# A recurrent-memory attention block with a SwiGLU gate, forward and backward: the phases around its two loops rebuilt

## The chip, the cores and the metric

The kernel runs on one core of a Trainium2 chip. The metric is device time in microseconds (us) from the first to the last instruction of one execution. A profile of an execution lists, for each engine, when it worked and what it waited for. The engines are TensorE (PE: matmuls; its weight loads are listed as PEld), VectorE (DVE), ScalarE (ACT), GpSimd (POOL) and SyncE (SP, which here only starts transfers). SBUF is the core's working memory with 128 partitions, PSUM the small memory into which PE writes, DRAM the large one outside. A DMA is a transfer between them; ACT, SP and POOL start the DMAs in this kernel.

## The reference

The reference computes an output and then, by automatic differentiation, the gradients of nine inputs, which are outputs too. The forward part, cut to what matters:

```python
xn = layernorm(x)                                   # x: 2048 tokens x 640
# A: 64 segments of 32 tokens, one after the other, 8 memory rows carried on
for s in range(64):
    h = concat([mem, xn[32*s:32*s+32]])             # 40 rows x 640
    q, k, v = h @ Wq, h @ Wk, h @ Wv                # 32 heads of 128: 4096 columns each
    p = softmax(mask(q @ k.T * scale))
    o = (p @ v) @ Wo                                # 40 x 640
    mem = o[:8]
    outs.append(o[8:])
s = concat(outs)
# B: SwiGLU, F = 1728
z = (silu(xn @ w1) * (xn @ w3)) @ w2
g = silu(z)
out = x + s * g
```

All inputs and outputs are bf16. The outputs are `out` and the gradients of x, mem0, Wq, Wk, Wv, Wo, w1, w3 and w2 for a given `grad_out` (G).

## The kernel before

The program is a row of phases, each with its own SBUF and PSUM pools. `k.dma` starts a DMA on SP and ACT in turn; `k.copy(..., eng='v' or 's')` copies on DVE or ACT. A pool's `bufs` is how many buffers a tile name rotates through.

```python
phase1_ln(k)          # LayerNorm; stores xn as rows (XN) and transposed (XNT)
phase2_Bfwd(k)        # SwiGLU forward; stores gate, up, h, z, g, G*g (GS), its transpose (GST)
phase3_Afwd(k)        # projections of the first tokens, then the forward loop over 64 segments
phase3b_out(k, out_0) # O projection of all tokens, out, and G*s (GG)
phase4_Abwd(k, out_2) # GO projection of the last tokens, a prologue, the backward loop over 64 segments
phase6_Awgrads(k, out_3, out_4, out_5, out_6)  # gradients of Wq, Wk, Wv, Wo; gradient of xn from attention
phase5_Bbwd_ln(k, out_1, out_7, out_8, out_9)  # SwiGLU backward, LayerNorm backward, gradients of w1, w3, w2
```

Phase 2, per chunk of 128 columns of F and 512 tokens:

```python
nc.scalar.activation(sig, pg, Sigmoid)          # pg, pu: PSUM, fp32
nc.vector.tensor_copy(gt, pg)
nc.scalar.copy(ut, pu)
nc.vector.tensor_tensor(sl, gt, sig, mult)
nc.vector.tensor_tensor(hBT[:, fc, :], sl, ut, mult)
k.dma(k.GATET[...], gt);  k.dma(k.UPT[...], ut)
# ... (z, g and the rows of h for each 128 tokens)
emit_wT_B(k, w1s, w3s, w2s, ps1, "pht")         # transposes of w1, w3, w2 through one PSUM buffer
```

Phase 3 begins by loading its four weights, projects 672 tokens, then loops; at the end of each segment the new memory, transposed, is stored element by element:

```python
for (W, src) in ((Wv, k.A_Wv), (Wk_, k.A_Wk), (Wq, k.A_Wq)):
    k.dma(W[:], src...)                          # 5.2 MB each
k.dma(Wo[:], k.A_Wo...)
for xt in range(6):                              # 112 tokens each
    for W in (Wv, Wk, Wq): ...                   # 8 banks of 512 columns, 5 matmuls each
# ... forward loop, at the end of segment t:
nc.gpsimd.dma_start(k.MTD[:, :, (t + 1) * 8:(t + 2) * 8], nxt[:, :, 0:8])
```

The O projection works tile by tile of 96 tokens, tokens as the stationary operand; the backward phase then loads its transposed weights and starts:

```python
for h in range(H):                               # 32 heads
    matmul(pa, oT[:, h, :], Wo[:, h, 0:512]);  matmul(pb, oT[:, h, :], Wo[:, h, 512:640])
# ... phase 4
k.dma(WoT[:], k.WOT...)                          # then WvT, WkT, WqT: 5.2 MB each
```

Phase 6, for 8 groups of 4 heads and 22 tiles of up to 120 rows (24 memory rows and 96 tokens):

```python
mem_rows(k, [(k.MTD, k.MR), (k.GMT, k.GMR)])     # memory rows turned back by PE
for qd in range(8):
    for tl in range(22):
        # loads of dS, P and the rows of k, q, g
        # transposes of dS (t6); three row gradients r6p -> gr (ACT, DVE, ACT)
        # their transposes t6g -> gT (ACT, DVE, ACT), then the gradient of xn:
        for i in range(3):
            for j in range(4):
                matmul(g5, gT[:, i, j, :], W[:, j, 0:512]);  matmul(g1, gT[:, i, j, :], W[:, j, 512:640])
        # acc[tile] += g5, g1 (DVE)
    for i in range(3):                           # gradients of Wv, Wk, Wq: 5 banks, 22 x 5 matmuls
        # ... always the same five PSUM banks
# then gWo: gow = rows(GMR, GS) in 44 loads; per group one load of orr; 704 pairs of matmuls
```

Phase 5:

```python
for ps_i in range(npass):                        # w2 gradients: 5 passes over all tokens
    for tt in range(16):
        k.dma(hb[...], k.HB[tt*128:(tt+1)*128])  # the rows of h loaded again in each pass
        # up to 6 matmuls
for fc in range(14):
    for blk in range(4):                         # 512 tokens
        # 5 matmuls -> pghb; loads of gate and up; 2 ACT and 7 DVE operations
        k.dma(GUPT[...], gupT);  k.dma(GGATET[...], ggT)
for tt in range(16):                             # loads of GGATET, GUPT; 56 pairs of matmuls; LayerNorm backward
    ...
for srcT in (GGATET, GUPT):                      # w1, w3 gradients: loaded again, transposed by PE, then matmuls
    ...
```

Of the kernel before, what the change touches and what calls it, by code (L numbers as in the profile page):

```python
# [40 lines left out]
class K:  # L41
# [110 lines left out]
    def setup_dram(self):  # L152
# [8 lines left out]
        self.GATET = mk("GATET", (self.FC * P, S))  # L161
        self.UPT = mk("UPT", (self.FC * P, S))
        self.HB = mk("HB", (S, self.FC * P))
        self.ZB = mk("ZB", (S, D))
# [3 lines left out]
        self.GG = mk("GG", (S, D))  # L168
        self.GXA = mk("GXA", (S, D))
# [20 lines left out]
        self.MTD = mk("MTD", (P, self.DC, T * 8))  # L190
        self.GMT = mk("GMT", (P, self.DC, T * 8))
        self.MR = mk("MR", (T * 8, D))
        self.GMR = mk("GMR", (T * 8, D))
# [25 lines left out]
    def tok_src(self, x0, nx, w, c0, c1):  # L219
# [4 lines left out]
        while a < nx:  # L224
            t, r = divmod(x0 + a - self.NB0, 24)
            if r == 0 and nx - a >= 48 and c1 - c0 <= 1024:
                nt = (nx - a) // 24
                out.append((a, a + 24 * nt, self.step_src(w, t, t + nt, 8, 32, c0, c1)))
                a += 24 * nt
            else:  # L230
                m = min(24 - r, nx - a)
                out.append((a, a + m, self.step_src(w, t, t + 1, 8 + r, 8 + r + m, c0, c1)))
                a += m
        return out
# [119 lines left out]

def fold_turn(k, bank, fs):
# [10 lines left out]
def phase3_Afwd(k):  # L366
    nc, tc = k.nc, k.tc
    D, DC, S, H, HD, T = k.D, k.DC, k.S, k.H, k.HD, k.T
    with tc.tile_pool(name="aw", bufs=1) as wp:
        Wv = wp.tile([P, DC, HD], BF16, name="Wv")  # L370
        Wk_ = wp.tile([P, DC, HD], BF16, name="Wk")
        Wq = wp.tile([P, DC, HD], BF16, name="Wq")
        Wo = wp.tile([P, H, D], BF16, name="Wo")
        for (W, src) in ((Wv, k.A_Wv), (Wk_, k.A_Wk), (Wq, k.A_Wq)):
            k.dma(W[:], src.rearrange("(dc p) h e -> p dc (h e)", p=P))
        k.dma(Wo[:], k.A_Wo.rearrange("h e d -> e h d"))


        units = wT_A_units(k, Wq, Wk_, Wv, Wo)
        with tc.tile_pool(name="b0", bufs=2) as io, tc.tile_pool(name="b0s", bufs=3) as stp, \  # L380
                tc.tile_pool(name="b0p", bufs=4, space=bass.MemoryType.PSUM) as ps, \
                tc.tile_pool(name="b0q", bufs=2, space=bass.MemoryType.PSUM) as ps2:
            ui = 0
            for xt in range(6):
                x0 = 112 * xt
                xs = io.tile([P, DC, 112], BF16, name="b0x", tag="b0x")
                nc.sync.dma_start(xs[:], k.XNT[:, x0:x0 + 112].rearrange("(dc p) t -> p dc t", p=P))
                for wi, (W, dst) in enumerate(((Wv, k.QVX[:, 1]), (Wk_, k.KX[:, :]), (Wq, k.QVX[:, 0]))):
                    for cg in range(4):
                        st = stp.tile([112, 1024], BF16, name="b0st", tag="b0st")  # L390
                        for b in range(2):
                            c0 = cg * 1024 + b * 512
                            pb = ps.tile([112, 512], F32, name="b0pb", tag="b0pb")
                            for dc in range(DC):
                                nc.tensor.matmul(pb[:], xs[:, dc, :], W[:, dc, c0:c0 + 512],
                                                 start=(dc == 0), stop=(dc == DC - 1))
                            k.copy(st[:, b * 512:(b + 1) * 512], pb[:], eng='vs'[b])
                        nc.sync.dma_start(dst[x0:x0 + 112, cg * 1024:(cg + 1) * 1024], st[:])
                        nu = ((xt * 12 + 4 * wi + cg + 1) * len(units)) // 72
                        while ui < nu:  # L400
                            units[ui](ps2, "wTps", stp)
                            ui += 1

        with tc.tile_pool(name="ast", bufs=1) as st, tc.tile_pool(name="achain", bufs=1) as ch, \
                tc.tile_pool(name="afill", bufs=1) as fl, \
                tc.tile_pool(name="aps", bufs=1, space=bass.MemoryType.PSUM) as ps, \
                tc.tile_pool(name="apm", bufs=1, space=bass.MemoryType.PSUM) as psm:
            kTs = [st.tile([P, H, 120], BF16, name=f"kT{i}") for i in range(2)]
            vt = st.tile([40, HD], BF16, name="vt")
            hxs = [st.tile([P, DC, 32], BF16, name=f"hx{i}") for i in range(2)]  # L410
            qTs = [st.tile([P, 4, P], BF16, name=f"xqT{i}") for i in range(2)]
            xPs = [st.tile([120, 4, P], BF16, name=f"xP{i}") for i in range(3)]
            PTs = [st.tile([120, 4, P], BF16, name=f"xPT{i}") for i in range(2)]
            for tt in kTs + hxs + qTs + xPs + PTs:
                nc.gpsimd.memset(tt[:], 0.0)
            bA, bB, bC = [psm.tile([P, 512], F32, name=f"bank{i}") for i in range(3)]
            pm = bA
            with nc.allow_non_contiguous_dma(reason="tiny mem0 transpose load"):
                for dc in range(DC):
                    nc.sync.dma_start(hxs[0][:, dc, 0:8], k.mem0[:, dc * P:(dc + 1) * P].rearrange("m p -> p m"))  # L420
                nc.sync.dma_start(k.MTD[:, :, 0:8], hxs[0][:, :, 0:8])
            rides = {}
            WARM = dict(G2=2, G3=1, G4=2, G5=2)

            def ride_ld(t):
                x0 = k.NB0 + 24 * t
                b, sub = t // 4, t % 4
                if sub == 0 and x0 < S:
                    w = min(96, S - x0)
                    rt = ch.tile([P, DC, 96], BF16, name="ride", tag="ride")  # L430
                    nc.sync.dma_start(rt[:, :, 0:w], k.XNT[:, x0:x0 + w].rearrange("(dc p) s -> p dc s", p=P))
                    rides[b] = (rt, w)

            def ride(t):
                x0 = k.NB0 + 24 * t
                if x0 >= S:
                    return
                b, sub = t // 4, t % 4
                rt, w = rides[b]
                r0 = 24 * sub  # L440
                r1 = min(r0 + 24, w)
                nc.gpsimd.tensor_copy(hxs[t % 2][:, :, 8:8 + r1 - r0], rt[:, :, r0:r1])

            def chain(t, gap):
                tl, s = t // 3, t % 3
                hx = hxs[t % 2]
                kT = kTs[tl % 2]

                def half(W, b, sg, eng):
                    bank = (bA, bB)[b]  # L450
                    packed_half(k, bank, hx, W, b)
                    k.copy(sg[:, b * 512:(b + 1) * 512], bank[:], eng=eng)
# [311 lines left out]
def phase4_Abwd(k, out2):  # L764
# [3 lines left out]
    with tc.tile_pool(name="gw", bufs=1) as wp:  # L768
# [27 lines left out]
        with tc.tile_pool(name="gst", bufs=1) as st, tc.tile_pool(name="gchain", bufs=1) as ch, \  # L796
# [25 lines left out]
            def ride_ld(t):  # L822
                if t < 8:
                    return
# [860 lines left out]
```

## Time and profile before

| what | value |
|---|---|
| time, median of 3 | 6446.4 us (6438.1 to 6450.8) |
| span of the profiled execution | 6484.5 us |
| granted PE clock, mean | 0.911 |
| forward loop with its tail | 614 to 1994 us |
| backward loop | 2436 to 3768 us |

The other phases, from the first and last start of their lines: LayerNorm 0 to 66, phase 2 from 66 to 281, weight transposes to 346, first projections 375 to 589, O projection 1994 to 2224, GO projection to 2327, prologue to 2436, phase 6 from 3848 to 5512, gWo 5546 to 5746, w2 gradients to 5999, SwiGLU backward to 6149, LayerNorm backward to 6287, w1 and w3 gradients to the end.

How to read the views. In a table of stretches, a row is a stretch of time with the busy time of each engine in it. In a list of waits, a row is "who waited <- for whom: us in total, times, longest". In a list of groups, a row is the source line, engine, operation, output<-input, shape and count, then "busy us, mean ns of one", then the idle time just before and what ended it. An engine's idle time costs something only where that engine sets the end of its stage. "L90" and "L92" are the two copy helpers, whatever phase they serve.

### The profile page before, as it was taken

The numbers are of one execution on the slowest core, as the hardware profiler recorded it, in microseconds if no ns is written. First come the engines' busy times: TensorE is split into PE (matmuls) and PEld (weight loads), VectorE is DVE, ScalarE is ACT, GpSimd is POOL, SyncE is SP. The second block draws the span as 40 slices with busy tenths as digits, with TensorE's granted clock in tenths as the row PEclk, the third lists the DMA queues.
The fourth block names the chain that finished last, engine by engine and source line by source line (L and its number), as shares of the span: only waits on it lengthen the run. The fifth ranks groups of instructions, "written<-read, shape, count | busy, mean of one in ns | idle before, by whom it ended". The sixth has DMA issues, their size and how long they took to land. (4 is left out here: it accounts for less than half of the span.)

```text
span 6484.5 us, 167849 instructions
## 1 busy us (share of the span) xinstructions
PE 5360.5 (83%) x68068; PEld 3158.2 (49%) x68620; DVE 2423.8 (37%) x7541; ACT 1896.1 (29%) x5180; POOL 990.0 (15%) x1507
## 2 busy tenths in 40 slices
PE   6868999999978748888889849889998999765698
PEld 3445555555545425555556525555555554432244
DVE  5423555555542124444444412322223222020852
ACT  3323455554542122322233212322223222010301
POOL 0000344343341012332333200000000000000000
PEclk9879999999988968998899969999999999875899
DMA  6474454444455555665566552332233222665673
GB/s 190 155 254 152 122 138 137 133 133 129 132 160 134 175 151 149 170 162 155 160 171 179 143 92 75 98 79 75 77 85 89 76 80 67 147 173 171 199 170 92
DMA packets 1053670, 880.57 MB, mean 136 GB/s; under 512 B 528584, under 2 KB 944168, under 8 KB 1046944
## 3 DMA queue, kind: packets, MB, share of 16 engines
q1 hardware_dynamic: 671546, 572.39, 31.8%
q10 hardware_dynamic: 337894, 213.14, 11.9%
q0 software_dynamic: 43456, 84.28, 5.1%
q8 instruction: 540, 8.85, 0.6%
q14 instruction: 234, 1.92, 0.1%
HBM read 560.29 MB, written 313.29 MB: 135 GB/s over the span
## 5 line engine op out<-in xcount | busy, mean ns | idle before, releaser
L1218 PE MATMUL wg<-gr,hr 120*128 120x512 bf16 (+1 forms) x2640 | 578.3, 379 | 0.8 <-DVE ghacc L1207 0.5
L1201 PE MATMUL g<-w,gT 128*128 128x512 bf16 x1936 | 572.2, 384 | 0.7 <-ACT gT L92 0.7
L1202 PE MATMUL g<-w,gT 128*128 128x128 bf16 x2112 | 466.2, 221 | 10.8 <-issue 1.9
L1218 PEld LDWEIGHTS <-hr 120*128 120x128 bf16 (+1 forms) x2640 | 254.0, 98 | 321.1 <-issue 22.1
L1207 DVE TENSOR_TENSOR ghacc<-ghacc,g 120x512 f32<-120x512 f32 (+1 forms) x154 | 105.8, 687 | 565.0 <-PE g L1201 565.0
L1201 PEld LDWEIGHTS <-gT 128*128 128x128 bf16 x2112 | 209.0, 99 | 220.1 <-issue 12.7
L339 PEld LDWEIGHTS <-gkv 128*8 128x8 bf16 x8192 | 213.0, 98 | 157.0 <-DVE gkv L880 34.5
L92 ACT COPY gT<-t6g 128x480 bf16<-128x480 bf16 (+1 forms) x352 | 191.7, 545 | 331.4 <-PE t6g L1192 208.6
L1211 POOL CAST gxo<-ghacc 120x640 bf16<-120x640 f32 (+1 forms) x22 | 15.8, 720 | 1589.4 <-issue 1477.8
L320 PEld LDWEIGHTS <-hx 128*32 128x32 bf16 x7680 | 177.7, 96 | 164.5 <-issue 3.9
L339 PE MATMUL gbank<-WvT,gkv 128*8 128x320 bf16 x4096 | 229.7, 401 | 27.4 <-DVE gkv L880 27.4
L90 DVE CAST stg<-bank 128x512 bf16<-128x512 f32 x256 | 177.1, 692 | 201.5 <-PE bank L320 195.0
L90 DVE CAST wgo<-wg 128x512 bf16<-128x512 f32 x72 | 47.5, 688 | 543.6 <-PE wg L1218 499.0
L606 ACT ACTIVATE xP<-xsp,xnm 120x120 bf16<-120x120 f32 (+1 forms) x704 | 239.8, 372 | 12.6 <-DVE xnm L602 7.0
L1243 PE MATMUL oa<-gow,orr 120*128 120x512 bf16 x704 | 197.2, 383 | 36.1 <-DMA orr<-OR 36.1
L1192 PE MATMUL t6g<-ident,gr 120*128 120x120 bf16 (+1 forms) x2112 | 188.1, 219 | 43.9 <-ACT gT L92 41.1
L992 POOL DMA_DIRECT2D VTD<-gvT x176 | 127.7, 727 | 539.9 <-ACT gvT L991 516.7
L1202 PEld LDWEIGHTS <-gT 128*128 128x128 bf16 x2112 | 208.6, 99 | 0.3
L92 ACT CAST wgo<-wg 128x512 bf16<-128x512 f32 x48 | 28.1, 585 | 582.8 <-PE wg L1218 533.6
L617 POOL TENSOR_TENSOR xP<-xP,xrz 120x480 bf16<-120x480 bf16 (+1 forms) x176 | 170.3, 967 | 163.5 <-ACT xP L606 115.4
L1476 PE MATMUL w2acc<-gzB_all,hb_tok 128*128 128x128 bf16 (+3 forms) x437 | 122.6, 435 | 85.2 <-DMA hb_tok<-HB 79.3
L1020 DVE SCALAR_TENSOR_TENSOR gdS<-gdp,Dx,gPr 120x120 bf16<-120x120 f32 (+1 forms) x704 | 188.8, 331 | 0.0
(314 smaller groups left out, 11496.1 us busy)
## 6 DMA issues: line engine op xcount, KB each, us to landing
QVS<-stg SPq DMA_DIRECT2D x128, 256.0 KB
gqv<-QVS SPq DMA_DIRECT2D x112, 192.0 KB
vTt<-VTD SPq DMA_DIRECT2D x64, 320.0 KB
OR<-xv POOLq DMA_DIRECT2D x168, 120.0 KB, 3.3
VTD<-gvT POOLq DMA_DIRECT2D x168, 120.0 KB, 5.1
orr<-OR SPq DMA_DIRECT2D x8, 2520.0 KB
PR<-xP POOLq DMA_DIRECT2D x168, 112.5 KB, 5.1
gPr<-PR SPq DMA_DIRECT2D x168, 112.5 KB
```

The source lines that it names most:

```text
L90: return nc.vector.tensor_copy(out, in_)
L92: return nc.scalar.copy(out, in_)
L320: k.nc.tensor.matmul(bank[32 * g:32 * g + 32, :], x[:, dc, :], W[:, dc, c0:c0 + 512], start=(dc == 0), stop=(dc == k.DC - 1), tile_positio ...
L339: k.nc.tensor.matmul(pm[p0:p0 + nq, 0:320], x[:, h, :], W[:, h, 320 * b:320 * b + 320], start=(first and i == 0), stop=(last and i == 15), ...
L606: nc.scalar.activation(Pb[0:n, j, 0:n], sp[0:n, j, :], ACT.Exp, bias=nmx[0:n, j:j + 1], scale=k.scale, accum_out=Z[0:n, j:j + 1])
L617: nc.gpsimd.tensor_tensor(Pb[0:n, :, 0:n], Pb[0:n, :, 0:n], bc_last(rz[0:n], n), ALU.mult)
L1020: nc.vector.scalar_tensor_tensor(dS[0:n, j, :], dp[0:n, j, :], Dx[0:n, j:j + 1], Pr[0:n, j, :], op0=ALU.subtract, op1=ALU.mult)
L1192: nc.tensor.transpose(pt[:, j, :], gr[0:n, i, j * P:(j + 1) * P], k.ident[0:n, 0:n])
L1201: nc.tensor.matmul(g5[:], gT[:, i, j, :], W[:, j, 0:512], start=f, stop=l)
L1202: nc.tensor.matmul(g1[:], gT[:, i, j, :], W[:, j, 512:640], start=f, stop=l)
L1218: nc.tensor.matmul(accs[dc][:], hr[0:n, tl, dc * P:(dc + 1) * P], grs[tl][0:n, 2 - i, :], start=(tl == 0), stop=(tl == NTL - 1))
L1243: nc.tensor.matmul(ac[j][0][:], lh, gow[0:n, tl, 0:512], start=(tl == 0), stop=(tl == NTL - 1))
```

## The change

The two loops keep their code. Around them:

- **Phase 2** stores what the backward needs, silu(gate) and d(silu)·up, in place of gate and up, so that the SwiGLU backward is two products. Wv is loaded while it runs. The weight transposes rotate over two PSUM buffers and four staging buffers.
- **Weights** share four SBUF buffers for the whole attention part. Wk, Wq and Wo are loaded while earlier projections run; WoT, WvT and WkT take the places of Wv, Wk and Wq around the O projection, WqT that of Wo at its end.
- **Memory rows** are stored as rows at the end of each segment, in arrays in the tile order of phase 6; nothing is turned back.
- **O projection**: blocks of 288 tokens as the moving operand, software-pipelined over groups of four heads; it also forms the gradient of z and its transpose.
- **Phase 6**: software-pipelined over tiles; the transposed row gradients go into a ring of 384 columns, from which full windows of 128 rows are multiplied; more PSUM banks rotate.
- **gWo**: 20 tiles of 128 rows in place of 22, after the loads of the next phase have been started.
- **Phase 5**: the rows of h and of the gradient of z stay in SBUF for the w2 gradients; SwiGLU backward, LayerNorm backward and the transposes run together per 256 tokens, and the rows for the w1 gradients stay in SBUF, those for w3 go through DRAM once.

The diff, cut to its core (`...` marks cuts):

```diff
@@ phase 2
-nc.vector.tensor_copy(gt, pg)
-nc.vector.tensor_tensor(sl, gt, sig, mult)
+nc.vector.tensor_tensor(sl, pg, sig, mult)
...
+nc.vector.scalar_tensor_tensor(ds, sig, 1.0, sl, op0=subtract, op1=mult)
+nc.vector.tensor_tensor(ds, sig, ds, subtract)
+nc.vector.tensor_tensor(ds, ds, ut, mult)
-k.dma(k.GATET[...], gt);  k.dma(k.UPT[...], ut)
+nc.sync.dma_start(k.SLT[...], sl);  nc.sync.dma_start(k.DUT[...], ds)
...
+nc.gpsimd.dma_start(Wv[:], k.A_Wv...)
-emit_wT_B(k, w1s, w3s, w2s, ps1, "pht")
+emit_wT_B(k, w1s, w3s, w2s, ps1, ("pht", "pz"))
@@ first projections
-for xt in range(6):
-    for W in (Wv, Wk, Wq): ...
+xs = load(XNT, 672 tokens);  load(Wk)
+for W in (Wv, Wk, Wq):          # Wq is loaded during Wv, Wo during Wk
+    for xt in range(6): ...
@@ end of a segment, both loops
-nc.gpsimd.dma_start(k.MTD[:, :, (t + 1) * 8:(t + 2) * 8], nxt[:, :, 0:8])
+fold_store(nc.gpsimd, k.m_rows(k.HRO, t + 1), fs)      # two DMAs of 8 x 320
@@ O projection
+nc.gpsimd.dma_start(WoT[:], ...);  ... WvT, WkT
-matmul(pa, oT[:, h, :], Wo[:, h, 0:512]);  matmul(pb, oT[:, h, :], Wo[:, h, 512:640])
+for i, (b, qd) in enumerate(work):
+    ld(*work[i + 2]);  turn(*work[i + 1]);  proj(b, qd)
+# proj: matmul(acc[dc], Wo[:, 4*qd+j, dc*128:(dc+1)*128], oT[:, j, 0:288])   5 x 4
+# turn: pt = ps.tile(..., tag="opt") with 2 buffers, 3 pieces
...
+nc.gpsimd.dma_start(WT["q"][:], k.WQT...)
@@ phase 6
-mem_rows(k, [(k.MTD, k.MR), (k.GMT, k.GMR)])
+for tl in range(NTL):
+    ld(u + 4);  s2(u + 2, 0);  s2(u + 2, 1);  s1(u + 3);  s3(u + 1, 0, 2)
+    s2(u + 2, 2);  s3(u + 1, 2, 3);  s4(u)
+# s1: transposes of dS; s2: row gradient i -> PSUM (2 banks rotate) -> gr (ACT, DVE, ACT)
+# s3: transposes of gr -> ring; s4: for each full window of 128 rows:
+#     for h in range(2): 12 x matmul(pg, ring[:, i, j, r0:r0+128], W[i][:, j, 320*h:320*h+320])
+# ld: per tile five DMAs on SP, three on ACT
+for i in range(3):
+    wg(qd, i);  next(h)          # 5 of 8 banks in rotation; the next group's first tiles in between
@@ gWo and phase 5
+for t0 in range(0, 16, 4):
+    nc.scalar.dma_start(gz[...], k.GZ[...]);  nc.scalar.dma_start(hb[...], k.HB[...])
+nc.scalar.dma_start(w2T[:], ...)
+phase6b_gWo(k, out6)             # orr on SP, gow on ACT; 1280 matmuls of 320 columns
...
-k.dma(hb[...], k.HB[...])        # in each of 5 passes
+# w2 gradients from hb, gz in SBUF: 4 groups of 7 banks
+nc.scalar.dma_start(xn_all[:], k.XN...)
+for b0 in range(0, 2048, 256):
+    gzT = load(GZT)
+    for fc in range(14):         # sl, du loaded two chunks at a time
+        # 5 matmuls -> pghb (2 PSUM buffers)
+        nc.vector.tensor_tensor(ggT[:, fc, :], pghb, du, mult)
+        nc.vector.tensor_tensor(guT[:, fc, :], pghb, sl, mult)
+    for ti in range(2):
+        # 56 matmuls of 320 columns, 28 transposes, LayerNorm backward
+# w1, w3 gradients: 640 matmuls of 432 columns
```

## Prediction

> **What bounds the kernel now.** I read the first row of the page, then the table of stretches cut at the first and last start of each phase's lines, then the waits inside the bad stretches, then the groups for prices.
>
> ```profile
> span 6484.5 us, 167849 instructions
> ...
> PE 5360.5 (83%) x68068; PEld 3158.2 (49%) x68620; DVE 2423.8 (37%) x7541; ACT 1896.1 (29%) x5180; POOL 990.0 (15%) x1507
> ```
>
> TensorE (PE) is the bound on average. The average hides where it is not. Columns of the table: stretch, length, then busy time of PE, weight loads, DVE, ACT, POOL, then granted clock, DMA share, GB/s.
>
> ```profile
> 281.00:346.00 65.00, 34.64 (x257) 24.29 (x255) 13.77 (x25) 16.32 (x28) 0.00 (x0) 0.58 0.36 120
> 346.00:375.00 29.00, 0.00 (x0) 0.00 (x0) 0.00 (x0) 0.07 (x1) 0.00 (x0) 0.50 0.92 375
> ...
> 2224.00:2327.00 103.00, 60.92 (x239) 26.02 (x243) 16.60 (x25) 13.73 (x24) 0.00 (x0) 0.78 0.77 265
> ...
> 3768.00:3848.00 80.00, 5.38 (x40) 4.16 (x40) 1.97 (x4) 2.77 (x4) 5.49 (x8) 0.51 0.89 113
> 3848.00:5512.00 1664.00, 1491.20 (x11616) 862.25 (x11792) 424.11 (x929) 415.27 (x773) 15.84 (x22) 0.98 0.30 81
> 5512.00:5546.00 34.00, 0.00 (x0) 0.00 (x0) 0.69 (x1) 0.58 (x1) 0.00 (x0) 0.53 0.94 214
> 5546.00:5746.00 200.00, 197.29 (x1408) 107.87 (x1408) 21.19 (x32) 8.43 (x32) 0.00 (x0) 0.99 0.55 118
> ...
> 5777.00:5999.00 222.00, 129.20 (x512) 50.13 (x522) 41.86 (x78) 18.09 (x35) 0.00 (x0) 0.58 0.60 185
> 5999.00:6149.00 150.00, 88.37 (x275) 32.68 (x280) 133.85 (x392) 60.61 (x113) 0.00 (x0) 0.81 0.66 201
> ```
>
> The reader is to see four kinds of loss: seams with PE nearly idle while data is loaded (346, 3768, 5512); a stage that starves on loads (5777, PE at clock 0.58); a stage bound by DVE (5999: DVE 134 of 150 us); and phase 6 at 3848, long and busy, with a small share lost in each of its 176 tiles. The waits name the causes:
>
> ```profile
> PE r6p L1181 <- ACT gr L1184: 51.4, 87, 0.7
> PE t6g L1192 <- ACT gT L92: 41.1, 72, 0.7
> ...
> PE w2acc L1476 <- DMA hb_tok<-HB: 79.3, 67, 4.5
> ...
> PE pghb L1491 <- ACT ghb L1500: 51.6, 40, 3.6
> ...
> PE mr_pt L1119 <- DMA mr_in<-MTD: 45.5, 1, 45.5
> ```
>
> The prices, mean ns of one just after "busy us,":
>
> ```profile
> L1201 PE MATMUL g<-w,gT 128*128 128x512 bf16 x1936 | 572.2, 384 | 0.7 <-ACT gT L92 0.7
> ...
> L880 DVE SCALAR_TENSOR_TENSOR gkv<-gbank,xp 128x256 bf16<-128x256 f32 x128 | 54.3, 424 | 266.4 <-ACT gOst L909 183.6 <-PE gbank L878 82.8
> L1366 DVE TENSOR_TENSOR sl<-gt,sig 128x512 bf16<-128x512 bf16 x52 | 22.0, 424 | 1.5
> ```
>
> The 384 ns of a matmul is not its cost, because matmuls overlap; the timeline shows a pair of 512 and 128 columns starting every 0.27 us.
>
> **What the Trainium skill says.** "TensorE: Matmul & The Clock Gate", section "Wait — 56ns, not 53.3ns?": warm matmuls start every N/2.4 ns plus about 2.5 ns. For the pair that is 215.8 + 55.8 = 271.6 ns, and the timeline's 0.27 us agrees, so I price PE work that way: 320 columns 135.8 ns, 120 columns 52.5 ns. The same page, "What's actually happening": an idle array falls back to half clock. The trace agrees: 0.50 to 0.58 in the seams, 0.98 in phase 6. "VectorE: DVE Perf Modes", "Why PSUM operands drop a tier": an fp32 operand in PSUM costs DVE its fast modes. The trace agrees: 256 columns from PSUM cost 424 ns, as much as 512 bf16 columns from SBUF. "DMA: Bandwidth & Descriptors", "Queues, rings and completion order": one issuing queue's descriptors are taken in ring order. No stretch shown here isolates it; I use it for the new seams.
>
> **The change part by part** (us of the profiled span; PE work priced as above).
>
> Phase 2 (66 to 281, 215). PE work stays at 199. DVE gains: per 128x512 chunk 0.69 + 0.42 + 0.68 + 0.42 + 0.42 = 2.63 (the 0.68 is a three-operand form, scaled from 0.82 for 640), times 56 is 147; per token tile 0.82 + 0.82 + 0.49 + 0.49 + 0.60 = 3.2, times 16 is 52. DVE then has 199 too, and the two don't mesh perfectly: 227, **+12**.
>
> Weight transposes and the load seam (281 to 375, 94). 42 groups now rotate over two PSUM buffers, about 0.7 each (copy 0.5 to 0.7 and two waits): 29; Wv is loaded under phase 2, so only the 0.9 MB of tokens remain ahead of the first projection, about 5, plus the ramp: 46, **-48**. The projections themselves, 720 x 215.8 ns + 640 x 55.8 ns = 191 at clock 0.95 plus 6: 207 against 214, **-7**. The loops (1380 and 1332) keep their code but for the memory stores: 0.
>
> O projection (1994 to 2224, 230). 1120 x 122.5 ns = 137, transposes 40, small ones 4: 181 at 0.98 is 185. Three transposed pieces share two PSUM buffers, so each of 49 turns waits about 0.35: 17. Sum 205. Its three weight swaps start already in the forward loop's tail, as the changed program's instruction order shows, so the GO stage (2224 to 2327, 103) has its 52 of PE and little else: 67. The prologue (109) starts with loads done: 100. Together 372 against 442, **-70**.
>
> Seam before phase 6 (80): the transposed memory rows are gone, a first tile's and weights' loads remain: 14, **-66**.
>
> Phase 6 (1664). Before: 2112 x 271.6 ns + 2640 x 215.8 ns + 262 for transposes and row gradients = 1405, so 259 lost. After: 20 full windows of 128 rows replace 22 tiles of up to 120, 3840 x 135.8 ns = 521, total 1354; at 0.985 that is 1374. The software pipeline leaves one exposed wait a tile, the row gradient that reuses a PSUM buffer while ACT copies (0.59 and two waits against 0.8 of PE work between): 0.15 x 176 = 26; seams between accumulations 15. Sum 1415, **-249**.
>
> Seam and stage of gWo (34 + 200). The loads of gz (2.6 MB), hb (7.1) and w2T (2.2) can start only when phase 6 lets its SBUF go, and gow stands behind them in the same queue. 1 KB rows: two orr tiles, gz and half of gow, 9.2 MB at the seam's own 214 GB/s = 43; 9.3 MB with 3456-byte rows at an estimated 320 (between 214 and the 375 of the Wv seam) = 29: a seam of 72. The matmuls, 1280 x 135.8 ns = 174, plus 4. Sum 250, **+16**.
>
> After 5746 (738.5). w2 gradients with everything in SBUF: 448 x 135.8 ns = 61, at 0.97 and four evictions 65. Then xn_all, 2.6 MB at 214 GB/s = 12, stands ahead of the first gzT: 16. SwiGLU with LayerNorm, 8 blocks: DVE needs 28 x 0.42 for the products, 4 x 0.53 for the copies and 2 x 3.2 (0.82 + 0.90 + 0.15 + 0.89 + 0.45) for LayerNorm = 20.3 a block, PE 25.9. In the chunk loop DVE is ahead (11.8), the remaining matmuls take 15.6, and some LayerNorm work falls into the next chunk loop: 28.5 x 8 = 228. w1/w3 gradients: 640 x 182.5 ns = 117, with clock and last store 127. Sum 436, **-302**.
>
> Sum: 12 - 48 - 7 - 70 - 66 - 249 + 16 - 302 = -714. 6484.5 - 714 = 5770 with the profiler, times 6446.4/6484.5 = 5736; I round to **5730**.
>
> **The rivals.**
> First, DVE and ACT become the bound in place of PE. For it: phase 2 and the SwiGLU chunk loop have DVE within some per cent of PE, and in phase 6 ACT has 0.59 + 0.60 + 1.0 = 2.2 us of copies a tile (the last scaled from 0.80 for 768 columns to 960) plus three DMA issues of 0.65, 4.15 of a 4.5 us tile. Against it: in the timeline DMA issue and ACT copies overlap. If ACT's two shares add up and wait in line, phase 6 ends near 1520 and the whole near 5840.
> Second, the transfers were moved, not removed: loads are put in large pieces on one queue, and what is needed first stands behind what is needed later. For it: the seam worked out above; the weights in the forward tail share engines with that tail's own loads. Against it: the big pieces have long rows. If each new seam is half as long again, +50: 5780.
> Third, the seams close better than I allow: the gWo loads overlap the last accumulations, the PSUM waits vanish. Phase 6 at 1375, SwiGLU at 212, that seam at 45, the prologue shorter: about -110: 5620.
> A slowdown would need the loops, untouched in code, to lose 700 us; nothing shown speaks for it.
>
> **Range and chances.** Terms of 20 to 40 us on phase 6, SwiGLU, the gWo seam, the O projection and phase 2, added as independent, give about 65; common errors in how I treat waits double that. So 5600 to 5860 for 8 times in 10. Faster by over 2%: 0.98; within 2%: 0.01; slower: 0.01.
>
> **What would show each step right or wrong.** Phase 6 from 1390 to 1440, PE over 0.95 busy in its tiles, and the largest PE wait the row gradients on ACT's copies; if it is 1500 or more with ACT near its limit, the first rival holds. A PE gap of 60 to 80 ahead of gWo that ends with the DMA into gow. w2 gradients of 65 with no wait for hb. Blocks of 27 to 30 in SwiGLU with DVE above 0.65 busy. Phase 2 longer than before with DVE above 0.85. Both loops within 15 of 1380 and 1332: if not, the sum fails in a place I left out.

## Result and profile after

| | median, us | ratio to the kernel before |
|---|---|---|
| kernel before | 6448.6 | 1 |
| changed kernel | 6008.2 (6003.2 to 6013.3) | 0.932, 95% interval 0.930 to 0.934 |

Faster by 6.8%; the prediction had 5730 us, and 6008 lies above its range. The kernel before took 6448 to 6483 us beside the various experiments, so these are compared by their ratio to it, and by the length of single stages in their traces. The changed kernel's 0.932 is the mark for all of them.

The first row of the page, for the changed kernel:

```profile
span 6007.0 us, 166595 instructions
...
PE 5182.7 (86%) x68354; PEld 3289.8 (55%) x68354; DVE 2394.8 (40%) x7496; ACT 1817.4 (30%) x4945; POOL 1038.9 (17%) x1654
```

The table of stretches, cut where its own stages begin (columns as above):

```profile
61.00:316.00 255.00, 221.69 (x1322) 116.52 (x1322) 176.79 (x362) 100.06 (x162) 2.30 (x3) 0.95 0.51 171
316.00:378.00 62.00, 24.86 (x220) 20.76 (x219) 9.86 (x18) 14.77 (x26) 1.17 (x2) 0.56 0.67 244
2003.00:2241.00 238.00, 197.93 (x2201) 160.87 (x2202) 88.86 (x232) 55.88 (x115) 20.13 (x22) 0.94 0.49 147
2241.00:2263.00 22.00, 0.25 (x5) 0.14 (x5) 0.00 (x0) 0.29 (x1) 0.88 (x1) 0.50 0.72 246
...
3747.00:3800.00 53.00, 12.19 (x108) 10.70 (x107) 6.97 (x18) 7.27 (x12) 3.02 (x6) 0.53 0.74 173
3800.00:5320.00 1520.00, 1420.36 (x11304) 914.11 (x11302) 440.76 (x947) 372.02 (x605) 0.00 (x0) 0.97 0.32 87
5320.00:5374.00 54.00, 0.25 (x2) 0.10 (x1) 1.46 (x3) 0.71 (x2) 0.00 (x0) 0.54 1.03 365
...
5551.00:5616.00 65.00, 64.55 (x448) 42.20 (x448) 6.65 (x15) 4.41 (x11) 0.00 (x0) 1.00 0.14 43
5630.00:5885.00 255.00, 239.88 (x1904) 164.39 (x1905) 144.42 (x351) 42.18 (x64) 20.98 (x15) 0.98 0.39 119
```

The w2 gradients are what was foreseen (65 us, PE busy throughout). But there are still stretches with PE nearly idle, at 316, 2241, 3747 and 5320, each with the DMA share at 0.67 or more; phase 6 has 100 us without PE work; and the stretches at 61 and 5630 hold more PE time than was priced. Phase 6 is the largest miss. The waits in it, first PE's longest, then ACT's on the same copy:

```profile
PE r6p L1273 <- ACT gr L1276: 38.7, 64, 2.2
```

```profile
ACT gr L1276 <- PE t L1261: 108.6, 35, 3.9
...
ACT gr L1276 <- DMA r<-GOS: 39.4, 17, 4.5
ACT gr L1276 <- DMA r<-QVS: 37.0, 15, 4.6
ACT gr L1276 <- DMA r<-GX: 34.5, 12, 3.5
```

PE waits for ACT's copy gr, and that copy seems to wait for loads into r and for transposes t. It reads neither: its only input is PSUM r6p. What waited were the DMA starts that stand ahead of it in ACT's program. The Trainium skill, "Perfetto Trace Analysis", section "DMA Instruction — HWDGE (DVE, Sync)", says that a start is reported only from when its semaphores are satisfied, so the wait before it has no row. Here that wait turns up as idle time of the next work: these 220 us on a copy that reads none of those tiles agree. The timeline of one tile shows the order:

```profile
4008.99 0.71 ACTq L1251 DMA_DIRECT2D r<-GOS  x1
4009.70 0.39 PE L1273 MATMUL r6p<-r,P 120*128 120x128 bf16 x4
4009.80 0.69 ACTq L1251 DMA_DIRECT2D r<-QVS  x1
...
4010.53 0.59 ACT L1276 CAST gr<-r6p 120x512 bf16<-120x512 f32 x1 [3.21 <-PE t L1261]
```

PE has r6p ready at 4010.1; ACT is still starting loads for a later tile, and copies at 4010.53.

### The profile page after: what moved, and what is told of

Same layout as the page of the kernel before. It is cut to its first block, busy times and chain, and to the rows that moved or that the text cites. A ratio compares the mean times of both kernels' runs of the same rounds, so it can differ in the third digit from the quotient of the medians.

```text
span 6007.0 us, 166595 instructions
## 1 busy us (share of the span) xinstructions
PE 5182.7 (86%) x68354; PEld 3289.8 (55%) x68354; DVE 2394.8 (40%) x7496; ACT 1817.4 (30%) x4945; POOL 1038.9 (17%) x1654
## 5 line engine op out<-in xcount | busy, mean ns | idle before, releaser
L1309 PE MATMUL g<-w,gT 128*128 128x320 bf16 x3840 | 555.6, 302 | 0.0
L1309 PEld LDWEIGHTS <-gT 128*128 128x128 bf16 x3840 | 372.2, 99 | 140.5
L1699 POOL TENSOR_TENSOR o<-gxn,ln_G 128x640 bf16<-128x640 f32 x16 | 22.4, 1398 | 2115.2 <-DVE gxn L1697 2115.2
L1276 ACT CAST gr<-r6p 120x512 bf16<-120x512 f32 (+1 forms) x176 | 103.1, 586 | 490.8 <-PE r6p L1273 202.1
L632 ACT ACTIVATE xP<-xsp,xnm 120x120 bf16<-120x120 f32 (+1 forms) x704 | 240.5, 376 | 10.4 <-DVE xnm L628 6.3
L1318 DVE TENSOR_TENSOR ghacc<-ghacc,g 128x320 f32<-128x320 f32 x240 | 117.0, 487 | 289.6 <-PE g L1309 289.6
L1419 PE MATMUL oa<-gow,orr 128*128 128x320 bf16 x1280 | 176.1, 301 | 54.3 <-DMA gow<-GWO 54.3
L662 ACT CAST xv<-xpo 120x512 bf16<-120x512 f32 (+1 forms) x176 | 103.3, 588 | 298.8 <-PE xpo L660 247.8
L92 ACT COPY gT<-t6g 128x960 bf16<-128x960 bf16 (+5 forms) x216 | 167.3, 794 | 57.3 <-PE t6g L1292 55.3
L1419 PEld LDWEIGHTS <-orr 128*128 128x128 bf16 x1280 | 126.0, 98 | 104.5 <-issue 54.7
L1112 DVE CUSTOM_DVE_ANT_0 gdS<-gdp,gPr 120x120 bf16<-120x120 f32 (+1 forms) x704 | 153.5, 273 | 60.6 <-PE gdp L1101 59.9
```

The lines of the kernel that those rows point to most:

```text
L92: return nc.scalar.copy(out, in_)
L632: nc.scalar.activation(Pb[0:n, j, 0:n], sp[0:n, j, :], ACT.Exp, bias=nmx[0:n, j:j + 1], scale=k.scale, accum_out=Z[0:n, j:j + 1])
L1112: nc.vector.tensor_tensor_reduce(dS[0:n, j, :], dp[0:n, j, :], Pr[0:n, j, :], 1.0, 0.0, ALU.mult, ALU.add, Dx[0:n, j:j + 1])
L1309: nc.tensor.matmul(pg[:], ring[:, i, j, r0:r0 + P], Ws[qd][i][:, j, 320 * h:320 * h + 320], start=(i == 0 and j == 0), stop=(i == 2 and j ...
L1419: nc.tensor.matmul(ac[j][i][:], orr[:, w, jj * P:(jj + 1) * P], gow[:, w, 320 * i:320 * i + 320], start=(w == 0), stop=(w == NW - 1))
```

## Experiments

The theories: A, the order of SP's queue holds loads back; B, ACT's loads stand in line with its copies; C, the 16 DMA engines are full of something that is not needed yet; and, for the front, the O projection and phase 5, waits on single buffers, DVE work and PE's own work. "Seam" is the time from the last matmul of one stage to the first of the next. A "tile window" is the time in phase 6 from the first matmul on one window of 128 rows to the first on the next. "Front" is the time from the start of phase 2 to the first projection. Each run numbers the lines of its own kernel, so a line of the same code can carry another number. A stage that an edit leaves alone still varies between traces: phase 6 took 1520 to 1532 us, the front 317 to 321, the O projection 237 to 239. The ratios are known to about 0.002 either way, some 13 us, so smaller effects are read from the stages alone.

### Phase 6: who starts the transfers

**e1_store.** The gradient stores.

```diff
-nc.sync.dma_start(outf[2 - i][...], ot)
+nc.gpsimd.dma_start(outf[2 - i][...], ot)
```

> One edit of the changed kernel: in phase 6 the stores of the gradients of Wq, Wk and Wv are started by POOL in place of SP. In the changed kernel 12.3 to 13.6 us pass in each of 7 seams from the last matmul of a weight-gradient pass to the first matmul of the next head group, and SP was held about 30 us by these stores ahead of the next tiles' loads. Theory A (SP's order holds back the loads): the seams fall to 3 to 5 us, phase 6 from 1520 to about 1455, whole 5940 to 5955. Theory B (ACT's DMA issues and copies in one line are what costs): seams and tiles stay, within 10 us of 6008. Theory C (the 16 DMA engines themselves are late, whoever starts the transfer): within 15 us of 6008.

Measured: 6029.1 us, ratio 0.931 (0.929 to 0.933); phase 6 1537 us, its seams 13 to 14. A falls as an account of the whole. SP was free, but in the same seam (three lines of the timeline, SP's load and ACT's load for the same tile):

```profile
3954.30 0.34 SPq L1244 DMA_DIRECT2D dS<-DSR  x1
...
3980.57 1.07 ACT L92 CAST wgo<-wg 128x512 bf16<-128x512 f32 x2 [24.82 <-PE wg L1331]
...
3981.80 0.66 ACTq L270 DMA_DIRECT2D r<-GOS  x1
```

ACT's part of the tile started 27 us later: ahead of it in ACT's order stood copies that waited 25 us for PE.

**e2_loads.** Three of a tile's eight loads.

```diff
-k.load_x(r, nm, src, nc.scalar if nm_ == "g" else nc.sync)
-(nc.sync if nm_ == "k" else nc.scalar).dma_start(r[0:nm, :], ...)
+k.load_x(r, nm, src, nc.gpsimd if nm_ == "g" else nc.sync)
+(nc.sync if nm_ == "k" else nc.gpsimd).dma_start(r[0:nm, :], ...)
```

> One edit of the changed kernel: of the eight loads of a tile in phase 6 the three that ACT starts are started by POOL. Theory B (ACT's issues stand in line with its copies, so the row gradient waits for the copy): tile windows fall from 5.03 to 5.28 us to about 4.85, phase 6 by 40 us, the seams of 12 to 14 us stay; whole about 5965. Theory A (SP's order): tiles may fall by 10 to 15 us in all, seams stay, whole 5990 to 6010. Theory C (the DMA engines): 6008 within 15.

Measured: 5962.3 us, ratio 0.920 (0.918 to 0.923). Phase 6 1476; tile windows 4.79 to 4.85 us in seven of eight groups; seams still 12 to 13. ACT now waits for PE alone:

```profile
ACT gr L1276 <- PE r6p L1273: 342.8, 148, 4.0
```

and PE's wait for it falls from 38.7 to 6.5 us; the stage's row stands below it:

```profile
PE r6p L1273 <- ACT gr L1276: 6.5, 11, 0.9
```

```profile
3797.00:5273.00 1476.00, 1406.19 (x11307) 908.44 (x11304) 440.12 (x947) 375.87 (x606) 293.95 (x509) 0.97 0.36 90
```

B holds, at 44 us of this stage (44 to 61 against the 1520 to 1537 that phase 6 took in the other runs in which ACT starts these loads). The seam before it shrank too, 52.5 to 41.5.

**e3_both.** Both edits.

> Both edits: the weight-gradient stores and ACT's three loads per tile in phase 6 are started by POOL. If A and B each explain their part, the gains add: seams 3 to 5 us, tiles 4.85 us, phase 6 about 1415, whole about 5900. If both now meet in POOL's queue, loads behind stores again, seams stay at 10 us or more and the whole is 5950 or more. Theory C: 6008 within 15.

Measured: 5972.3 us, ratio 0.922 (0.920 to 0.924); phase 6 1494. They meet in POOL's queue:

```profile
3978.91 0.54 POOL L1336 DMA_DIRECT2D out_dram<-wgo  x1 [1.17 <-DVE wgo L90]
3979.52 0.69 POOL L270 DMA_DIRECT2D r<-GOS  x1
```

The load of the next group stands behind the last store again. A queue is not relieved by moving both of its customers.

**e12_early** (with e2 and e9). The fourth tile of the next group is loaded ahead of the last five stores on SP.

```diff
 for i in range(3):
     s2(u0, i)
+ld(u0 + 3)
 s1(u0 + 1)
 yield                        # the third weight-gradient pass and its stores
 s3(u0, 0, 2);  s3(u0, 2, 3)
-ld(u0 + 3)
```

> e9_hrlate with the loads of the fourth tile of each next head group started one weight-gradient pass earlier, ahead of that pass's five output stores on SP. The seams between groups stayed 12.5 to 13 us in all three of e1, e2 and e3, with PE busy 8 of them. Theory A' (part of it is the fourth tile's load behind the stores): seams fall by 2 to 4 us each, phase 6 by 15 to 25, whole 15 to 25 below e9_hrlate. Theory E (the seam is the fill of the software pipeline, copies and clock, whatever the loads): seams stay within 1 us, whole within 8 of e9_hrlate.

Measured: 5928.0 us, ratio 0.914 (0.912 to 0.917). Seams 8.1 to 10.2 in place of 12.4 to 13.8, phase 6 1462 against 1492 in e9. So A' holds: with B out of the way SP's order does cost 3 to 4 us a seam. The rest of a seam is work: in two seams of the changed kernel PE was busy 8.3 and 7.3 us of 13.6 and 12.3, filling the pipeline.

### The seam before phase 6: what fills the DMA engines

**e4_hr.** Both loads of hr, the rows that the weight gradients of phase 6 multiply.

```diff
-nc.scalar.dma_start(hr[...], k.HRO[...])
+nc.gpsimd.dma_start(hr[...], k.HRO[...])
```

> One edit: the two loads of hr at the start of phase 6 are started by POOL in place of ACT. In the changed kernel the seam ahead of phase 6 lasts 56 us and ACT's first copy of a row gradient comes at 36 us of it, after ACT's queue had stood at the second hr load. Theory A/B (the issuing engine's order): the seam falls to 30 to 38 us, whole about 5985. Theory C (the loads themselves take that long): the seam stays at 50 to 56, whole 6008 within 10.

Measured: 6028.9 us, ratio 0.931 (0.929 to 0.933); seam 50.4. Who starts hr does not matter.

**e9_hrlate** (with e2). The loads of hr move into the tile loop.

```diff
-nc.scalar.dma_start(hr[...], k.HRO[...])                     # ahead of the loop
+if u == 5:
+    nc.gpsimd.dma_start(hr[...], k.HRO[...])
```

> e2_loads (the three loads per tile on POOL) with hr, 3.2 MB that is first needed about 100 us later, loaded after tile 5 of the first group. In e2_loads the seam from the last matmul of the backward loop to the first matmul of phase 6 took 41.5 us; in the changed kernel the DMA engines were over 0.9 busy from 17 to 35 us of that seam. Theory C for this seam (the engines are full of what is not yet needed): 6 in place of 9 MB, the seam falls by 12 to 18 us, to 24 to 30, whole about 15 us below e2_loads. Theory D (round trips of the first tiles' own small loads): the seam stays at 38 or more.

Measured: 5963.3 us, ratio 0.920 (0.918 to 0.922). The seam falls from 41.5 to 27.8, so C holds there; but the whole gains nothing. One tile window took 17.2 us:

```profile
3812.45 0.66 POOL L270 DMA_DIRECT2D r<-GOS  x1 [14.46 <-DMA hr<-HRO]
```

The tiles' loads waited for hr in the middle of the stage in place of its start: moved, not gained. In e14_all hr comes in eight pieces over 16 tiles, and the first group's mean window is 5.19 in place of 5.52, where the six groups after it have 4.79: splitting took away about half of that stall.

### O projection and GO stage

**e6_op.** Two transposed pieces in one PSUM tile.

```diff
-pt = ps.tile([P, 4, nx], BF16, tag="opt")
+if t != 1:
+    pt2 = ps.tile([P, 2, 4, nx], BF16, tag="opt")
+pt = pt2[:, t % 2]
```

> One edit of the changed kernel: in the O projection the first two of three transposed pieces share one PSUM bank, so the third piece finds a free bank and no longer waits for a copy of the first. The stage takes 234 us, with 27 us of PE waits on those copies, 20 of its 21 tiles in blocks of three. Theory 1 (the PSUM wait is what holds it): stage 207 to 215, whole about 22 us less. Theory 2 (ACT, which starts the four loads of the epilogue in line with its copies and waits for their landing): stage within 6 us of 234.

Measured: 6065.3 us, ratio 0.940 (0.938 to 0.942); the stage took 285 us in place of 238. The edit was badly chosen: the second piece's transposes now waited for the copy of the first out of the same tile. The waits of the changed kernel, then of this one:

```profile
PE opt L782 <- ACT oT L92: 15.4, 19, 0.9
PE opt L782 <- DVE oT L90: 11.7, 36, 0.5
```

```profile
PE opt L784 <- DVE oT L90: 70.7, 56, 2.9
```

44 us more of this wait, 47 more of the stage: the stage follows it one to one.

**e10_turn.** All work kept, only PE's order changed:

```diff
-turn(*work[i + 1]);  proj(b, qd)
+turn(*work[i + 1], (0, 1));  proj(b, qd, (0, 1, 2))     # 12 of 20 matmuls
+turn(*work[i + 1], (2,));    proj(b, qd, (3, 4))
```

> One edit of the changed kernel: in the O projection PE transposes the third piece of the next item after 12 of the 20 matmuls of this one, so that the copy of the first piece has long freed its PSUM bank; all work stays. e6_op, where two pieces shared a bank, waited more on the copies (71 us against 27) and its stage took 280 in place of 234. Theory 1 (these PSUM waits set the stage): waits on copies fall to under 8 us, stage 208 to 215, whole about 22 us less. Theory 2 (ACT's epilogue line or the loads of orow take over as the bound): waits move to the small transposes or to orow, stage 225 or more.

Measured: 5991.2 us, ratio 0.924 (0.921 to 0.926); stage 208.1 in place of 238.2.

```profile
PE opt L786 <- ACT oT L92: 0.3, 1, 0.3
```

That is what is left of the 15.4 us on ACT; the 11.7 on DVE went to 0.2. The 27 us of waits are gone and the stage is 30 shorter. Theory 1 holds.

**e7_gzt.** The stores of GZT.

```diff
-nc.gpsimd.dma_start(k.GZT[...], gzT)
+nc.scalar.dma_start(k.GZT[...], gzT)
```

> One edit of the changed kernel: the stores of the transposed gradient of z in the O projection are started by ACT in place of POOL. After the O projection PE idles 26 us; the last such store was issued by POOL right behind the 5.2 MB load of WqT, the copy ahead of it waited 17.7 us for the store before, and the next stage's first load came at the end of all. Theory 1 (the store stands in POOL's queue behind WqT): the gap falls to 6 to 10 us, whole about 17 us less. Theory 2 (the transfers of 5.2 MB fill the DMA engines, whoever starts the store): the gap stays at 20 or more. The O projection itself may gain or lose 3 us.

Measured: 6012.3 us, ratio 0.932 (0.930 to 0.933); gap 18.0 in place of 22.0.

```profile
2239.61 0.38 ACTq L844 DMA_DIRECT2D GZT<-ep_gzT  x1
2253.86 0.96 SPq L884 DMA_DIRECT2D g0x<-GST  x2
```

The store starts at once from another queue, but the next stage's first load, whose SBUF it holds, starts 14 us later, when the 5 MB of WqT are through. That is theory 2, though its "20 or more" was a little high. The Trainium skill, "DMA: Bandwidth & Descriptors", section "Issuing engines are not separate DMA queues", says that all transfers share the 16 engines whoever starts them, so that spreading them saves only issue time. This gap agrees: another starter saved 4 of 22 us. In e2_loads the starter decided 44 us or more, but not through the transfers: there its waits held up its other work.

**e11_wqt.** WqT after the next stage's loads, in SP's order.

```diff
-nc.gpsimd.dma_start(WqT, k.WQT...)       # end of the O projection
+for x0 in ...:                            # GO stage
+    nc.sync.dma_start(xs[x0], k.GST[...])
+nc.sync.dma_start(WqT, k.WQT...)
```

> One edit of the changed kernel: WqT, 5.2 MB, is loaded after the first loads of the GO stage, and those are all started at its beginning. In e7_gzt the gap ahead of the GO stage still took 18 us, with the last small store issued at once but landed only when the 5.2 MB were through. Theory C (the engines are full of WqT, and the next stage's SBUF waits for the small store): gap 5 to 9 us in place of 22 (first matmul after the last transposes), whole 12 to 17 us less, unless the prologue then waits for WqT. Theory of queue order: e7_gzt took that away and gained 4, so nothing more is to be had: gap 18 or more.

Measured: 6025.8 us, ratio 0.929 (0.927 to 0.932). Gap 6.9, but the GO stage 63 in place of 55: 7 net. The prologue did not change (107.6).

### gWo

**e8_gow.** The order of ACT's loads: gow for gWo, gz, hb and w2T for the stages after it.

```diff
-load(gz), load(hb), load(w2T), load(gow)
+load(gow), load(gz), load(hb), load(w2T)
```

> One edit of the changed kernel: ACT starts the loads of gow ahead of those of gz, hb and w2T. The seam ahead of gWo takes 54 us at 365 GB/s; it ends when gow has landed. Theory 1 (gow stands behind 12 MB in its queue): only gow (3.3 MB) and the first orr tiles (5.2 MB) remain ahead of the first matmul, 8.5 MB at 365 GB/s, so the seam falls to 23 to 30 us, the stages after it stay, whole about 27 us less. Theory 2 (moved, not gained): gWo then waits for later orr tiles or the w2 gradients wait for hb, and the whole stays within 8 us.

Measured: 6001.3 us, ratio 0.930 (0.928 to 0.931). Seam 25.4 in place of 54.3, gWo 192.8 in place of 176.1: 12 net. PE waited once, 14.2 us, for a copy whose buffer was held by an output store that now ran beside those loads. Both theories are half right.

### The front, and PE's own work

**e5_p2.** Work left out.

```diff
-scalar_tensor_tensor(ds, sig, 1.0, sl, ...);  tensor_tensor(ds, sig, ds, subtract);  tensor_tensor(ds, ds, ut, mult)
+ds = ut
```

The three DVE operations on ds are left out and ut is stored in its place (what is built on that derivative is then not the reference's).

> The changed kernel with the three DVE operations that form the derivative in phase 2 left out, and the copy of up stored in its place (the SwiGLU gradients are then not the reference's; every transfer and all PE work stay). Phase 2 takes 241 us there with DVE busy 171 and PE 214. Theory 1 (DVE's added work delays PE): DVE falls to about 86, phase 2 to 215 to 222, whole 20 to 25 us less than the changed kernel. Theory 2 (PE's own work at clock 0.95 and waits for store buffers): phase 2 stays at 234 to 241 and the whole within 8 us.

Measured: 6005.2 us, ratio 0.931 (0.929 to 0.933). Phase 2 with its tail ended 7 us earlier, the front is 310 in place of 317. DVE's added work was worth 7 us, and not the 20 to 25 of theory 1.

**e13_pad.** The 64 rows of the last chunk of F are padded with zeros to 128 where they are contracted or transposed, here and likewise in phase 2.

```diff
-matmul(pgx[:, h, 0:320], gT[0:fsz, fc, tcol], wT[0:fsz, fc, ...])
-transpose(pt[:, fc * P:fc * P + fsz], gT[0:fsz, fc, tcol], ident[0:fsz, 0:fsz])
+matmul(pgx[:, h, 0:320], gT[:, fc, tcol], wT[:, fc, ...])
+transpose(pt[:, fc * P:fc * P + P], gT[:, fc, tcol], ident)
```

> One edit of the changed kernel: the last chunk of F, 64 rows, is padded with zeros to 128 rows where it is contracted or transposed (z matmuls and h transposes in phase 2; xn-gradient matmuls and transposes in the SwiGLU backward); the sums are the same. In the changed kernel's trace a 320-column matmul over 64 rows starts 0.231 us before the next, and the one after it 0.239, against 0.136 between two over 128 rows: about 0.2 us for each chunk of 64 rows. Theory F (the change of the number of rows costs PE, and that is why the SwiGLU stage had 240 us of PE work and not 207): per 256 tokens 8 matmuls x 0.2 and 4 transposes x 0.17, 2.3 us, times 8 is 18; in phase 2 32 x 0.2 and 16 x 0.17, 9. SwiGLU stage 255 to about 237, phase 2 241 to about 232, whole about 25 us less. Rival (DVE's products and LayerNorm set the SwiGLU stage, the clock the rest): SwiGLU within 4 of 255, phase 2 within 3, whole within 8.

Measured: 6007.6 us, ratio 0.929 (0.927 to 0.931). SwiGLU 245.7 in place of 255.3, phase 2 with its tail 4 us shorter. In the timeline a run of 14 matmuls of 320 columns, the last of them over 64 rows in the changed kernel; the next run's start ends its cost. Changed kernel, then padded:

```profile
5753.19 2.18 PE L1671 MATMUL pgxb<-w3T,guT 128*128 128x320 bf16 x14
5755.31 1.03 PE L1678 MATMUL ptt<-ident,ggT 128*128 128x128 bf16 x14
```

```profile
5747.65 2.06 PE L1676 MATMUL pgxb<-w3T,guT 128*128 128x320 bf16 x14
5749.55 0.94 PE L1683 MATMUL ptt<-ident,ggT 128*128 128x128 bf16 x14
```

2.12 us from start to start against 1.90, which is 14 x 0.1358. PE's work in the stage fell by 16 us (239.9 to 223.9), as F has it; the stage fell by 10, because waits for DVE grew (for ggT from 4.4 to 10.4 us). So F and its rival share the term.

**e15_bufs.** More buffers for what is stored.

```diff
-sl, ds: bufs=2;  wTB_st: bufs=4
+sl, ds: bufs=5;  wTB_st: bufs=7
```

> The changed kernel with more buffers for what phase 2 stores: sl and ds rotate through 5 in place of 2, the staging tiles of the weight transposes through 7 in place of 4. In the changed kernel PE waited 10.4 and 7.1 us at 70 to 95 us for DVE, which waited for the stores of sl and ds, while Wv (5.2 MB) was being loaded; and 14.7 us at 330 us for a staging tile's store. Theory G (a store that is late holds its buffer, and through it DVE and PE): the last pg matmul comes at about 259 in place of 275, the stretch from 61 us to the first projection 317 falls to 285 to 295, whole about 25 us less. Rival (the engines are too full for the stores at any depth, so the wait only comes some chunks later): the stretch stays at 308 or more.

Measured: 5996.6 us, ratio 0.927 (0.926 to 0.928). PE's wait for sl fell from 17.5 to 8.8 us and phase 2 ended 10 us earlier, but the first projection still came 318 us after its start: its load of tokens ran beside 5 MB weights either way. The projections took 217 in place of 237, and 16 us of waits for their staging tiles vanished; front and projections together are 18 us shorter. G is shown in phase 2. The staging tiles of the projections are not those that the edit multiplied, so how the 20 us come from it stays open.

**e16_pgs.** Another PSUM buffer.

```diff
-pgs = ps1.tile([P, DC, P], BF16, tag="pz")
+pgs = ps1.tile([P, DC, P], BF16, tag="pht")
```

> One word of the changed kernel: in phase 2 the transposes of the gated gradient (pgs) share a PSUM buffer with the h transposes (pht) in place of z (pz). In the tail of phase 2 three token tiles take 10.1 us each, with PE idle 2 to 3 us twice and pz of the next tile waiting until the copy of pgs has freed the buffer. Theory H (that one buffer's chain of activation, two products, transposes, copy is what the tail costs): tiles 10.1 to about 7.5, the stretch from 61 us to the first projection about 9 less, whole 6 to 10 less. Rival (the h transposes then wait in its place): within 3.

Measured: 6012.6 us, ratio 0.930 (0.928 to 0.931); the front 313 in place of 317. Neither theory's numbers; the intervals of the ratios overlap, so this run does not tell it from the changed kernel.

### Together

**e14_all**: e2, e12, hr in eight pieces, e10, e11, e8, e13.

> All that helped together: the three loads per tile on POOL, the fourth tile's loads earlier, hr in eight pieces during the first group in place of one, the third transposed piece of the O projection after 12 matmuls, WqT after the GO stage's loads, gow ahead of gz and hb, the 64 rows padded. If the causes are separate and add: phase 6 with its seam 1576 to about 1480 (after: 3744 to 5320), O projection and gap to the GO stage 260 to about 215, GO stage 55 to 63, gWo with its seam 231 to about 219, SwiGLU 255 to 237, phase 2 241 to 232: sum about -185, whole about 5825. If the gains sit on each other (loads on POOL against hr and each other, or the clock gives back what PE gains), 5860 or more.

Measured: 5865.0 us, ratio 0.906 (0.904 to 0.908), so 2.8% under the changed kernel (0.9056/0.9319 = 0.972), or 169 us at its 6008. The time alone lies past the 5860 of the rival, gains that sit on each other; but the kernel before took 6475 beside this run and 6449 beside the changed kernel, so the ratio and the stages decide. Phase 6, from the table of stretches:

```profile
3722.00:5180.00 1458.00, 1396.12 (x11314) 899.32 (x11313) 439.53 (x947) 375.67 (x606) 299.23 (x515) 0.98 0.37 93
```

Phase 6 with its seam took 1488 (expected 1480), O projection and gap 216 (215), GO stage 64 (55 to 63), gWo with its seam 218 (219), SwiGLU 246 (237); the front is 6 shorter (9). So the causes add, to within 16 us of the 185 expected, and most of what is missing is in SwiGLU and phase 6. This is the fastest version run; e15's buffers, tried after it, are not in it.

## Why the prediction was wrong

Stage by stage in us of the traces, from the start of phase 2; the last column is e14_all.

| stage | predicted | changed kernel | all edits |
|---|---|---|---|
| phase 2, transposes, load seam | 273 | 317 | 311 |
| first projections, forward loop | 1612 | 1625 | 1623 |
| O projection | 205 | 238 | 209 |
| gap and GO stage | 67 | 77 | 71 |
| prologue | 100 | 108 | 105 |
| backward loop | 1332 | 1321 | 1313 |
| seam before phase 6 | 14 | 53 | 30 |
| phase 6 | 1415 | 1520 | 1458 |
| seam and stage of gWo | 250 | 230 | 218 |
| w2 gradients, next seam | 81 | 79 | 79 |
| SwiGLU, LayerNorm | 228 | 255 | 246 |
| w1/w3 gradients | 127 | 121 | 123 |

The mechanism of the gain was right: -714 was predicted for the span, 6484.5 - 6007.0 = 477 came, but of the parts that were to shrink four did not, or hardly: the front (309 us before, from 66 to 375, and 317 after), the first projections (214 and 213), the O projection (230 and 238) and the prologue (109 and 108). The loops stayed within 15 us as said. Point by point:

- **Phase 6, +105.** The step that failed is "in the timeline DMA issue and ACT copies overlap", with which the first rival was set aside. They do overlap in part while both run; what was overlooked is that ACT takes them in order, and a start waits for a buffer and for earlier landings, and the copy behind it with it: without these starts on ACT the stage took 1476 (e2). The rival's own figure for the stage, 1520, is what came, and its "wait in line" is what was seen, but the match of the figure is luck: it stood on ACT being near its limit, 4.15 of 4.5 us a tile. From the first gradient of xn to the first weight gradient of each group, 808 us in all, ACT's copies took 302 us and its starts, which the profile does not count as busy, 265, together 526 with their overlap. e2 gave 44 of the 105. e12 took 30 off the stage as e9 had it, 26 of them in the seams: the term "seams between accumulations 15" was mis-sized, since seven seams of 12.3 to 13.6 are some 91 us, of which PE was busy about 8 each. The rest is PE itself: 1354 was priced at clock 0.985, 1374; in e12 and e14_all PE was busy 1393 and 1396.
- **Seam before phase 6, +39.** "a first tile's and weights' loads remain: 14" left out hr and the order in which ACT takes its starts. Without the tiles' loads on ACT the seam fell by 11 (e2), with hr later as well by a further 14 to 28 (e9). The other 14 are not taken apart.
- **O projection, +33.** The form was right, "each of 49 turns waits about 0.35: 17", but the term was mis-sized: the waits were 27 us, and the stage fell by 30 when they went (e10). PE's work was mis-sized too, 198 us busy where 185 was priced. The other 10 are not taken apart; 3 of the predicted 205 are a slip, since 185 + 17 is 202.
- **GO stage, +10.** "Its 52 of PE and little else" was right of the stage (55). The gap ahead of it, 22, was the second rival: WqT, not needed yet, on the DMA engines. Loading it later gave 7 net.
- **Prologue, +8.** "The prologue (109) starts with loads done" did not come true: PE waited 51.5 us there for its own small loads (of gqv, 18 times). No run changes that.
- **gWo, -20.** "9.2 MB at the seam's own 214 GB/s" was too slow: the seam moved its bytes at 365 GB/s, and took 54, not 72. That it ends with gow, which stands behind the other loads, was right: with gow first it took 25 (e8).
- **Phase 2 and the front, +44.** Phase 2 took 255 where 227 was predicted, transposes and load seam 62 where 46 was. "DVE then has 199 too" named the wrong bound: DVE was busy 177, and taking away its added work gave 7. Late stores holding two buffers cost phase 2 another 10 (e15), the 64-row chunk 4 (e13); the three make 21 of the 28 if they add, which no run shows. In the seam, "about 5" for the tokens was mis-sized: their load was started at 363.0 us, those of Wk and Wq, 5.2 MB each, within 0.5 us of it, and PE waited until 378.2:

```profile
378.23 7.03 PE L422 MATMUL b0pb<-Wv,b0x 128*112 128x512 bf16 x24 [13.39 <-DMA b0x<-XNT]
```

That the weights held up the tokens is read from the trace; no run changes their order. The 13 us of the table's second row are the loop's 8, inside the 15 allowed, and most of the 7 that the first projections were to gain.

- **SwiGLU, +27.** "PE 25.9" per block of 256 tokens priced all matmuls alike. PE was busy 240 where 8 x 25.9 = 207 had been priced. The change between 128 and 64 rows is 16 of these 33, and the stage gave back 10 when it was gone; the other 17 are not taken apart. The waits were no larger than in the sum, 15 against 21 (228 - 207).

So the size of the whole was missed because many terms were too small, some in PE's own work and more in the waits around it, and nearly all in the same direction (only gWo, the backward loop and the gradients of w1, w2 and w3 came out shorter): the range treated them as independent.

## What to carry to other kernels

An engine that copies PSUM for PE should not start loads whose buffers come free late: the wait of a start has no row of its own, and shows as a copy that "waits" for tiles it doesn't read. When a seam is full of transfers, ask which of its bytes are needed first; a large load that is only moved can make the same stall elsewhere (hr cost one tile window 17.2 us in e9), and splitting it into eight took away about half of that here. When PE needs a third PSUM buffer and there are two, put other matmuls in between before looking for a bank.

## What the runs showed of the hardware

- A matmul over 64 rows between matmuls over 128 cost about 0.2 us more than one over 128: matmuls of 320 columns start 0.231 and 0.239 us apart around it, 0.136 elsewhere; padded with zeros it cost as much as the others (e13).
- PE's transposes into one half of a PSUM tile waited for DVE's copy out of its other half, in this program: 71 us in 56 waits (e6). Whether the program's waits or the memory demands that, the run does not tell.
- POOL could start the tiles' loads without holding anything up, as long as nothing else stood in its queue: with them it was busy 294 of 1476 us, and the tile windows fell to 4.8 us (e2). Behind hr (e9) or behind the stores (e3) the same loads came late.
